# Sums of exponentials in free PSUM columns, pre-scaled keys, and a new order list, in an attention kernel with two feed-forward layers

## Chip, cores and metric

One core of one Trainium2 chip. The metric is the device time of one execution in microseconds; the median of the runs counts.

## What is computed

Attention over 2 batches of 8 heads, 768 positions of width 64, then two feed-forward layers on the 1536 rows of 512 that come out of it. Each query sees the keys less than 16 positions away, and besides them 24 summaries, one for each block of 32 keys (maximum of the keys, mean of the values):

```python
scale = 1.0 / np.sqrt(D)
k_sum = k.reshape(B, H, nb, block, D).max(axis=3)
v_sum = v.reshape(B, H, nb, block, D).mean(axis=3)
scores_l = scale * np.matmul(q, k.transpose(0, 1, 3, 2))
scores_s = scale * np.einsum('bhsd,bhnd->bhsn', q, k_sum) + np.log(block)
scores_all = np.concatenate([np.where(mask_l, scores_l, -1e9), scores_s], axis=-1)
a = np.exp(scores_all - np.max(scores_all, axis=-1, keepdims=True))
a = a / (np.sum(a, axis=-1, keepdims=True) + 1e-09)
x = np.matmul(a, np.concatenate([v, v_sum], axis=2))   # then heads side by side: 1536 x 512
h = x @ w_in;  x = (h * np.cos(h)) @ w_out              # first layer, 2048 wide
h = x @ w_in2; x = (h * np.clip(h + 3, 0, 6) / 6) @ w_out2
```

## The kernel before

The kernel is written as a graph of about 2,600 operations. `G.op` (L169) notes for each operation the engines that may do it, keys that it reads and writes, and a function that issues its instructions. `G.run` (L191) issues them in the order of `ORDER` (L39), a list written out in the file: `p118` puts operation 118 on TensorE's queue, `a` stands for ScalarE, `v` for VectorE, `g` for GpSimd, `s` for SP (which issues all DMAs). A `+2` puts two filler matmuls of zeros behind an operation (`fill`, L1028); `ws` and `we` load the tables for sine and exponential. Each engine works through its queue in order and waits there for what an instruction needs. The numbers are those of the graph, so a step that is added or removed renumbers what follows.

Attention runs in 12 units of 128 queries (`front`, L617, and `back`, L704). For a unit, with its 8 heads in two banks of PSUM (4 heads of 120 columns in each: 96 keys of the window, 24 summaries; 480 of a bank's 512 columns):

- masks (L633, an identity times the mask, on TensorE) or, from unit 7 on, a seed (a copy of the mask by ScalarE or VectorE, L443) fill the two banks; scores are added on top (L656; for units 0 to 3, called direct, straight from the keys, L658 and L660). Units 1 and 3 use banks a0 and a1, the others c0 and c1.
- largest (L684, VectorE): the maximum of each head; negative (L614 on VectorE, L612 on ScalarE): times minus the scale
- power (L693, ScalarE): eight exponentials of 120 columns, each with bias nmx and the scale, each followed by a reading of the accumulator into `sm`, which is the sum
- sum (L698), inverse (L700, both VectorE), scaled (L701, GpSimd or VectorE)
- flip (L723, transposes on TensorE), flipped (L443, a copy out of the bank), weighted (L739, times the values), x hi (L443) and x lo (L756): the result as two numbers of reduced precision
- units 0 and 1 take the first of these steps in two halves.

From unit 4 on the keys are not read from `ktile` but from `kcat`, into which window (L443) copies the keys of the unit's two windows and put k (L550) the summaries. The summaries of v are made by means (L579) and copied by put v (L443). Values of a window come by load window (L746).

The feed-forward layers take their weights as 64-bit floats; carry (L505, L507), rebias (L514), shift (L517), join (L519), hi (L443) and lo (L460) turn each slice of 512 KB into two 32-bit parts. A product is three matmuls (hi hi, hi lo, lo hi): first (L933) makes h, middle steps (L1009 to L1024) the gate, second (L1064) the second product. The first steps of the first layer run between the units of attention, 256 rows at a time; later steps take products in blocks (L881).

## Time and profile before

| | us |
|---|---|
| median of 3 runs | 569.22 (568.99 to 569.26) |
| the profiled execution, its own time | 570.81 |
| span of that execution, first to last instruction | 569.0 |
| TensorE busy in the span | 559.9 |
| VectorE / ScalarE / GpSimd busy | 460.6 / 341.4 / 231.3 |

Times of the trace are microseconds from the start of the span. PE is TensorE, PEld its weight loads, DVE is VectorE, ACT ScalarE, POOL GpSimd, SP SyncE. A busy TensorE is modelled from pipelined matmuls, so a matmul's row is longer than its share of the pipeline.

### The profile page before, as it was taken

The numbers are of one execution on the slowest core, as the hardware profiler recorded it, in microseconds if no ns is written. First come the engines' busy times: TensorE is split into PE (matmuls) and PEld (weight loads), VectorE is DVE, ScalarE is ACT, GpSimd is POOL, SyncE is SP. The second block draws the span as 40 slices with busy tenths as digits, with TensorE's granted clock in tenths as the row PEclk, the third lists the DMA queues.
The fourth block names the chain that finished last, engine by engine and source line by source line (L and its number), as shares of the span: only waits on it lengthen the run. The fifth ranks groups of instructions, "written<-read, shape, count | busy, mean of one in ns | idle before, by whom it ended". The sixth has DMA issues, their size and how long they took to land.

```text
span 569.0 us, 9914 instructions
## 1 busy us (share of the span) xinstructions
PE 559.9 (98%) x3736; PEld 477.4 (84%) x3736; DVE 460.6 (81%) x853; ACT 341.4 (60%) x730; POOL 231.3 (41%) x230
## 2 busy tenths in 40 slices
PE   9999999999999999999999999999999999999997
PEld 6688999888888888888888888888888889888885
DVE  5888897698999898978899998867778687766653
ACT  4989997757547786765668677655643443422130
POOL 4788756856524214435263453032132303132111
PEclk9999999999999999999999999999999999999999
DMA  8998525223012211233200222224203220200013
GB/s 299 285 259 279 161 67 177 76 74 101 11 39 74 75 38 38 75 116 105 75 2 0 75 74 75 75 74 149 74 7 130 87 74 2 75 1 1 29 46 149
DMA packets 17232, 51.49 MB, mean 90 GB/s; under 512 B 1952, under 2 KB 2464, under 8 KB 17184
## 3 DMA queue, kind: packets, MB, share of 16 engines
q1 hardware_dynamic: 17184, 50.86, 26.8%
q8 instruction: 29, 0.48, 0.3%
q14 instruction: 19, 0.16, 0.1%
HBM read 47.71 MB, written 3.15 MB: 89 GB/s over the span
## 4 chain that ended last, share of the span: by engine, by line
PE 92%; DMA 4%; DVE 2%; SPq 1%; issue 1%; ACT 0%; DVEq 0%; ACTq 0%
PE bank_a L1064 25%; PE bank_d L881 15%; PE bank_b L1064 11%; PE bank_c L1064 11%; PE bank_e L881 9%; PE bank_c L881 8%; PE bank_d L933 4%; PE bank_e L933 2%; DMA vcats<-in_vw_dram 2%; PE bank_c L933 1%; PE bank_b L739 1%; PE bank_b L723 1%; PE bank_c L656 1%; DMA raw<-in_w_in_dram 1%; DMA qt<-in_q_dram 1%
## 5 line engine op out<-in xcount | busy, mean ns | idle before, releaser
L514 ACT ACTIVATE cv_t<-raw 128x512 f32<-128x512 f32 x64 | 42.6, 674 | 21.2 <-POOL plo L460 7.6
L519 POOL TENSOR_TENSOR cv_y<-cv_t,cv_y 128x512 int32<-128x512 int32 x24 | 33.2, 1386 | 37.4 <-ACT cv_y L505 18.9
L443 ACT CAST ghi<-hs 128x512 fp32r<-128x512 f32 x44 | 27.2, 618 | 23.4 <-DVE hs L1020 12.8
L1024 POOL TENSOR_TENSOR glo<-ch_c,ghi 128x512 fp32r<-128x512 f32 x12 | 16.9, 1405 | 52.2 <-ACT ghi L443 43.9
L1024 DVE TENSOR_TENSOR glo<-hs,ghi 128x512 fp32r<-128x512 f32 x46 | 34.8, 758 | 3.4 <-ACT ghi L443 2.7
L505 ACT ACTIVATE cv_y<-raw 128x512 int32<-128x512 uint32 x47 | 31.0, 670 | 8.5 <-POOL plo L460 4.2
L517 DVE TENSOR_SCALAR cv_t<-cv_t 128x512 int32<-128x512 int32 x64 | 27.9, 440 | 4.1 <-ACT cv_t L514 3.8
L460 POOL TENSOR_TENSOR plo<-cv_y,phi 128x512 fp32r<-128x512 f32 (+1 forms) x15 | 17.2, 1150 | 32.2 <-ACT phi L443 32.1
L519 DVE CUSTOM_DVE_ANT_0 cv_y<-cv_t,cv_y 128x1024 uint16<-128x1024 uint16 x40 | 28.0, 706 | 1.2 <-ACT cv_y L505 1.1
L693 ACT ACTIVATE es<-bank_c,nmx 128x120 f32<-128x120 f32 x80 | 27.6, 370 | 1.9 <-DVE nmx L614 1.7
L881 PE MATMUL bank_d<-xlo,phi 128*128 128x256 f32 (+1 forms) x106 | 26.3, 329 | 0.0
L881 PE MATMUL bank_d<-xhi,plo 128*128 128x256 f32 (+1 forms) x106 | 26.2, 329 | 0.0
L881 PE MATMUL bank_d<-xhi,phi 128*128 128x256 f32 (+1 forms) x106 | 26.2, 328 | 0.0
L701 POOL TENSOR_TENSOR es<-es,rs 128x960 f32<-128x960 f32 (+1 forms) x14 | 21.9, 1565 | 9.1 <-DVE rs L700 8.5
L443 ACT CAST ghi<-ch_c 128x512 fp32r<-128x512 f32 x26 | 16.1, 618 | 12.9 <-DVE ch_c L1020 7.1
L897 DVE TENSOR_TENSOR ch_c<-bank_d,ch_c 128x256 f32<-128x256 f32 (+1 forms) x31 | 14.2, 462 | 10.4 <-PE bank_d L881 8.7
L1111 DVE SCALAR_TENSOR_TENSOR total<-bank_a,total 128x512 f32<-128x512 f32 x28 | 19.0, 686 | 3.3 <-PE bank_a L1064 3.3
L1024 POOL TENSOR_TENSOR glo<-hs,ghi 128x512 fp32r<-128x512 f32 x7 | 10.2, 1457 | 27.4 <-DVE ghi L443 12.4
L1064 PE MATMUL bank_a<-ghi,whi_out 128*128 128x512 f32 x60 | 21.3, 390 | 0.0
L1064 PE MATMUL bank_a<-ghi,wlo_out 128*128 128x512 f32 x60 | 21.3, 389 | 0.0
L1064 PE MATMUL bank_a<-glo,whi_out 128*128 128x512 f32 x60 | 21.2, 389 | 0.0
L881 PEld LDWEIGHTS bank_d<-xhi,phi 128*128 128x128 f32 x106 | 18.8, 189 | 2.8
(391 smaller groups left out, 1966.7 us busy)
## 6 DMA issues: line engine op xcount, KB each, us to landing
raw<-in_w_in_dram SPq DMA_DIRECT2D x32, 512.0 KB, 3.3
raw<-in_w_out_dram SPq DMA_DIRECT2D x32, 512.0 KB, 3.3
vcats<-in_vw_dram SPq DMA_DIRECT2D x12, 384.0 KB, 5.7
qt<-in_q_dram SPq DMA_DIRECT2D x12, 256.0 KB, 6.1
ktile<-in_kt_dram SPq DMA_DIRECT2D x7, 384.0 KB, 6.0
total<-in_vw_dram SPq DMA_DIRECT2D x8, 256.0 KB, 4.7
out_dram<-total SPq DMA_DIRECT2D x8, 256.0 KB, 2.1
vnat<-in_vw_dram SPq DMA_DIRECT2D x4, 256.0 KB, 5.5
```

Of the source, the lines that this page charges most:

```text
L443: nc.scalar.copy(o, i) if e == "ACT" else VEC[e].tensor_copy(o, i)
L505: nc.scalar.activation(y, low.bitcast(U32), AF.Copy, scale=2.0 ** -29)
L514: nc.scalar.activation(o, a, AF.Prelu, scale=2.0 ** -112, alpha=-2.0 ** 32)
L517: G.op("shift", {"DVE": dve(DM, 2)}, lambda e: nc.vector.tensor_scalar(t, t, 3, None, ALU.logical_shift_left), w=[tk], twice=True)
L519: G.op("join", {"POOL": pool(DM), "DVE": dve(DM)}, lambda e: VEC[e].tensor_tensor(y, t, y, ALU.add), r=[tk], w=[yk], twice=True)
L693: nc.scalar.activation(ef[:, j, hp], s4[j][:, hp, :], AF.Exp, bias=nmx[:, j, hp:hp + 1], scale=scale, accum_out=sm[:, j, hp:hp + 1])
L701: G.op("scaled", {"POOL": pool(2 * nz * KC, 1.25) - 0.07, "DVE": dve(2 * nz * KC)}, lambda e, ef=ef, rs=rs, nz=nz: VEC[e].tensor_tensor(ef ...
L881: nc.tensor.matmul(o, wt[i][:, A[a], kk * P:(kk + 1) * P], xt[:, kk, :], start=first and p + kk == 0, stop=p + kk == 3, skip_group_check=True)
L933: nc.tensor.matmul(h, w["in"][i][:, kk * P:(kk + 1) * P], x[blk][:, kk, c0:c1], start=p + kk == 0, stop=p == 2 and kk == NK - 1)
L1024: G.op("g lo", {"DVE": dve(N), "POOL": pool(N)}, lambda e: VEC[e].tensor_tensor(gbuf("lo", s)[:, 0:N], c(), gh().bitcast(F32), ALU.subtrac ...
L1064: nc.tensor.matmul(acc(s, i)[0], l, r, start=first, stop=end and p == 2 and (N == TOK or i % 2 == 1), skip_group_check=N < TOK)
L1111: G.op("sums", {"DVE": dve(TOK)}, lambda e: nc.vector.scalar_tensor_tensor(t(), a, 1.0 / 6.0 if m else 1.0, t(), ALU.mult, ALU.add), r=[ak ...
```

## The change

The scale of 1/8 moves. For units from 4 on the keys (window and put k), the seeds and the identity of the masks (`eighth`, `eighths`, two new tiles made by ScalarE) carry it; `largest` gives the negated maximum at once, `negative` is gone, and `power` uses scale 1. Units 0 to 3 keep their form. For all units `sm` is no longer a tile in SBUF: it is 8 columns of the second score bank, from column 480 + 8 x (unit modulo 2), so the accumulator's readings go to PSUM and `sum` reads them there. The keys of the graph for `sm` and for the bank stay separate. The graph has 2 operations more at the start and 8 fewer later, and `ORDER` is a new list. Its first lines, of 125 before and 124 after:

```diff
-    s6 p4 s5 s17 s7 g2 a3 a1 v11 s34 s9 p18+2 v10 s60 s8 v0 s283 p19 p35+3 v20 v12 a21 p36+1 s61 a22 v14 s290 v37 p66
-    s51 g119 v13 p26 a38 a39 p27+2 v23 v24 v284 s82 g25 v28 a285 p43 v29 p44 v286 s297 a30 v40 v287 p74 s62 p67+1 v45
-    g288 s64 p52 v31 a46 v75 g289 p53+1 s63 a47 v32 v41 s65 g33 a292 v54 p83 s99 g42 a299 p84 s78 v48 a55 v298 a56 v49
-    v300 p68 s95 g50 v85 p76 p69 p70+1 g101 v77 p71 s117 g15 p91 v86 g301 v72 a87 s311 p100 p102 g16 v57 v58 p79 v103
-    g59 a92 p93+2 v80 s113 a104 s138 a105 v94 g73 p109+2 v81 s136 g302 v110 p96 v293 v88 v303 s135 p111 a313 v89 p118
-    v312 a97 v314 p120 a112 v106 g315 v98 s137 a291 p114 v121 g90 s131 a316 p353 v142 a115 p365 p354 a122 s145 p366 p355
...
+    s8 p6+1 s7 s19 s10 s36 s11 s62 s9 g2 s277 v13 a4 a5 a3 s63 v12 a1 p20 s64 v0 p37 p21+2 s53 v22 s67 p38+1 v15 a23 a24
+    v39 p68+3 v16 v14 g103 a40 p28+1 a41 v25 v120 p29 v26 a278 p45 g27 v30 a279 p69 p46 v31 v42 s291 v280 a32 p70 v43
+    s84 v281 p76+2 s65 v47 g282 s66 a77 p54 s101 v44 a48 p55 s80 a49 g17 v283 g18 p93 v56 s118 a292 p85 s97 a293 p86 v33
+    v57 v34 s305 v294 a58 v35 p71 g295 v87 p72 p73 p78+3 v50 v88 v51 a296 g52 p102 a79 p104+5 v59 a89 g297 v74 v60 v105
+    p81 g61 p95+2 v94 a82 s114 v96 s284 g75 a106 p110+2 s137 v83 s136 v90 s138 p98 v91 v111 g92 p112 a99 s131 p119 v113
+    s135 a307 p347 s145 v100 p359 p348 p121 v306 v107 v308 v108 a285 g309 p115 v122 p360 a116 v310 p349 p361 v141 a286
...
```

Under the operations' names the queues are the same behind TensorE's 253rd, ScalarE's 321st, VectorE's 187th, GpSimd's 69th and SP's 51st operation of the new list. Ahead of that the places and, for some sixty operations, the engine differ. GpSimd has 12 operations fewer, ScalarE 6 more, VectorE as many as before. Where the steps below speak of one queue, these are its operations in their order, with the numbers of the old graph:

```text
SP before:    ... 61 load v, 290 weights, 51 load q, 82 load q, 297 weights, 62, 64, 63, 65 load v, 99 load q, 78, 95 load window,
              117 load q, 311 weights, 113 load window, 138, 136, 135, 137 load k, 131 load window, 145 load q, 304 weights, ...
SP after:     ... 61, 62 load v, 51 load q, 65 load v, 297 weights, 82 load q, 63, 64 load v, 99 load q, 78 load window, 117 load q,
              95 load window, 311 weights, 113 load window, 290 weights, 137, 136, 138 load k, 131 load window, 135 load k, ...
PE before:    ... 100 masks (unit 4), 102 scores, 79 weighted (unit 0), 93 flip+2, 109 flip+2, 96 weighted (unit 1), ...
PE after:     ... 76 flip+3, 100 masks (unit 4), 102 scores+5, 79 weighted (unit 0), 93 flip+2, 109 flip+2, 96 weighted (unit 1), ...
DVE before:   ... 85 largest, 77 flipped, 86 negative, 72 put v, 57 sum (unit 2), 58 inverse, 103 largest (unit 4), ...
DVE after:    ... 85 largest, 48 sum, 86 negative, 49 inverse, 57 sum (unit 2), 72 put v, 58 inverse, 103 largest (unit 4), ...
list after:   ... v57 behind p102;  v124 (sum, unit 5) between p146 and p148 (masks and scores, unit 6);
              v188 (sum, unit 8) behind a214 (seed, unit 9);  v238 (sum, unit 10) behind p252 (scores, unit 11) ...
```

The rest of the diff:

```diff
@@ -372,7 +371,7 @@
     qt = ring(kv, "qt", NQ, [P, HP, P])
     es = ring(kv, "es", NE, [P, 2, HP, KC])
     pts = ring(kv, "pts", 2, [KC, H, P])
-    small = {n: ring(kv, n, 2, [P, H]) for n in ("mx", "nmx", "sm", "sme", "rs")}
+    small = {n: ring(kv, n, 2, [P, H]) for n in ("mx", "nmx", "sme", "rs")}
 
 
     zero = const.tile([P, P], F32R, name="zero")
@@ -428,6 +427,10 @@
     both = [ident[:, c:c + QH].unsqueeze(1).to_broadcast([P, 2, QH]) for c in (0, QH)]
     G.op("identities", {"POOL": pool(P)}, lambda e: nc.gpsimd.tensor_tensor(
         twice.rearrange("p (a c) -> p a c", a=2), *both, ALU.add), w=["twice"], at=CONST, twice=True)
+    eighth = kv.tile([P, P], F32R, name="eighth")
+    eighths = kv.tile([P, P], F32R, name="eighths")
+    G.op("identity", {"ACT": act(P)}, lambda e: nc.scalar.mul(eighth, ident, scale), w=["eighth"], at=CONST)
+    G.op("identity", {"ACT": act(P)}, lambda e: nc.scalar.mul(eighths, twice.bitcast(F32), scale), r=["twice"], w=["eighths"], at=CONST)
     G.op("mask", {"ACT": act(3 * KC)}, lambda e: nc.scalar.copy(mask_hi, mask), w=["mask_hi"], at=CONST)
 
 
@@ -547,8 +550,8 @@
 
     def put_k(b, i):
         n = HP * 2 * NB
-        G.op("put k", {"DVE": dve(n, 2), "POOL": one(n)}, lambda e: VEC[e].tensor_copy(
-            kcat[i][:, :, :, WK:KC], ksum[b].unsqueeze(2).to_broadcast([P, HP, 2, NB])
+        G.op("put k", {"DVE": dve(n, 2), "POOL": one(n)}, lambda e: scaled_copy(
+            e, kcat[i][:, :, :, WK:KC], ksum[b].unsqueeze(2).to_broadcast([P, HP, 2, NB])
         ), r=[("ks", b, hp, c0) for hp, c0, _ in pieces(b)], w=[("kcs", i)], twice=True)
 
     def vstage(t):
@@ -612,6 +615,12 @@
             nc.scalar.activation(o, i, AF.Copy, scale=-scale)
         else:
             nc.vector.tensor_scalar(o, i, -scale, None, ALU.mult)
+
+    def scaled_copy(e, o, i):
+        if e == "ACT":
+            nc.scalar.activation(o, i, AF.Copy, scale=scale)
+        else:
+            VEC[e].tensor_scalar(o, i, scale, 1.0, ALU.mult, ALU.mult)
 
     def front(u):
         b, tb = divmod(u, TB)
@@ -627,22 +636,25 @@
             sp = [bank[n][:, 0:nz * KC] for n in spk]
             s4 = [x.rearrange("p (h c) -> p h c", h=nz) for x in sp]
 
-            def masks(e, sp=sp, nz=nz):
+            same = (twice if direct else eighths) if m == 1 else (ident_r if direct else eighth)
+
+            def masks(e, sp=sp, nz=nz, same=same):
                 for j in range(2):
                     js = slice(QH * j, QH * (j + 1)) if m == 1 else slice(0, P)
                     nc.tensor.matmul(
-                        sp[j], (twice if m == 1 else ident_r)[js], mask_hi[js, m, :].unsqueeze(1).to_broadcast(
+                        sp[j], same[js], mask_hi[js, m, :].unsqueeze(1).to_broadcast(
                             [js.stop - js.start, nz, KC]), start=True, stop=False)
 
             seeded = u >= SEEDED
             if seeded:
                 def seed(e, sp=sp, nz=nz):
                     for j in range(2):
-                        copy(e, sp[j].rearrange("p (h c) -> p h c", h=nz), mask_hi.bitcast(F32)[:, m, :].unsqueeze(1).to_broadcast([P, nz, KC]))
+                        scaled_copy(e, sp[j].rearrange("p (h c) -> p h c", h=nz), mask_hi.bitcast(F32)[:, m, :].unsqueeze(1).to_broadcast([P, nz, KC]))
 
                 G.op("seed", {"ACT": 2 * act(nz * KC), "DVE": 2 * dve(nz * KC)}, seed, r=["mask_hi"], w=spk)
             else:
-                G.op("masks", {"PE": 0.41 if m == 1 else 0.5}, masks, r=["mask_hi", "twice", "ident_r"], w=spk)
+                G.op("masks", {"PE": 0.41 if m == 1 else 0.5}, masks, r=["mask_hi", "twice", "ident_r"] if direct else [
+                    "mask_hi", "eighth", "eighths"], w=spk)
 
             def scores(e, s4=s4, z0=z0, z1=z1):
                 for part in range(2 if direct else 1):
@@ -668,33 +680,36 @@
                     ap=[list(ktile[0].ap[0]), [S, nz], [a[1] - a[0], 2], [1, WK]],
                 )
                 n = nz * 2 * WK
-                G.op("window", {"ACT": act(n), "DVE": 0.55, "POOL": one(n)}, lambda e, keys=keys: copy(
+                G.op("window", {"ACT": act(n), "DVE": 0.55, "POOL": one(n)}, lambda e, keys=keys: scaled_copy(
                     e, kc[:, :, :, 0:WK], keys), r=[x for hp in range(HP) for x in kkeys(hp)], w=[("kcw", k)], twice=True)
                 G.op("scores", {"PE": 0.98}, scores, r=[("qt", qi), ("kcs", k), ("kcw", k)], w=spk)
             ef = es[ei][:, :, z0:z1, :]
             gs = [g] if first else [0, 1]
-            mx, nmx, sm, sme, rs = (small[n][si].rearrange("p (j h) -> p j h", j=2)[:, :, z0:z1]
-                                    for n in ("mx", "nmx", "sm", "sme", "rs"))
+            mx, nmx, sme, rs = (small[n][si].rearrange("p (j h) -> p j h", j=2)[:, :, z0:z1]
+                                for n in ("mx", "nmx", "sme", "rs"))
+            c = HP * KC + H * si
+            sm = bank[spk[1]][:, c:c + H].rearrange("p (j h) -> p j h", j=2)[:, :, z0:z1]
 
             def key(n):
                 return [(n, si, x) for x in gs]
 
             def largest(e, mx=mx, s4=s4):
                 for j in range(2):
-                    nc.vector.tensor_reduce(mx[:, j], s4[j], AX.X, ALU.max)
-
-            G.op("largest", {"DVE": dve(2 * nz * KC) + 0.07}, largest, r=spk, w=key("max"))
-            G.op("negative", {"DVE": 0.1, "ACT": 0.2}, lambda e, nmx=nmx, mx=mx: negate(e, nmx, mx),
-                 r=key("max"), w=key("mx"), twice=True)
+                    nc.vector.tensor_reduce((mx if direct else nmx)[:, j], s4[j], AX.X, ALU.max, negate=not direct)
+
+            G.op("largest", {"DVE": dve(2 * nz * KC) + 0.07}, largest, r=spk, w=key("max" if direct else "mx"))
+            if direct:
+                G.op("negative", {"DVE": 0.1, "ACT": 0.2}, lambda e, nmx=nmx, mx=mx: negate(e, nmx, mx),
+                     r=key("max"), w=key("mx"), twice=True)
 
             def power(e, ef=ef, s4=s4, nmx=nmx, sm=sm, nz=nz):
                 for j in range(2):
                     for hp in range(nz):
-                        nc.scalar.activation(ef[:, j, hp], s4[j][:, hp, :], AF.Exp, bias=nmx[:, j, hp:hp + 1], scale=scale,
+                        nc.scalar.activation(ef[:, j, hp], s4[j][:, hp, :], AF.Exp, bias=nmx[:, j, hp:hp + 1], scale=scale if direct else 1.0,
                                              accum_out=sm[:, j, hp:hp + 1])
 
             ek = [("e", ei, x) for x in gs]
-            G.op("power", {"ACT": 2.75 * nz / HP}, power, r=key("mx") + spk, w=ek + key("sm"), table="exp")
+            G.op("power", {"ACT": 2.47 * nz / HP}, power, r=key("mx") + spk, w=ek + key("sm"), table="exp")
             G.op("sum", {"DVE": 0.13}, lambda e, sme=sme, sm=sm: nc.vector.tensor_scalar(sme, sm, 1.0e-9, None, ALU.add),
                  r=key("sm"), w=key("sme"), twice=True)
             G.op("inverse", {"DVE": 0.17}, lambda e, rs=rs, sme=sme: nc.vector.reciprocal(rs, sme), r=key("sme"), w=key("rs"))
```

## Rows read from the trace of the kernel before

**Rows 1.** Busy time, share of the span and instructions of each engine (page)

```profile
PE 559.9 (98%) x3736; PEld 477.4 (84%) x3736; DVE 460.6 (81%) x853; ACT 341.4 (60%) x730; POOL 231.3 (41%) x230
```

**Rows 2.** Table by stretches: length, busy us per engine (instructions), clock, DMA share, GB/s

```profile
core 0: us, PE busy (x) PEld busy (x) DVE busy (x) ACT busy (x) POOL busy (x), PEclk, DMA share, GB/s
...
20.00:30.00 10.00, 9.26 (x173) 6.90 (x169) 9.17 (x23) 9.13 (x46) 6.45 (x9) 1.00 0.91 265
30.00:40.00 10.00, 8.85 (x154) 7.98 (x143) 8.61 (x17) 8.55 (x29) 9.85 (x9) 1.00 0.90 248
...
60.00:70.00 10.00, 10.00 (x151) 9.24 (x151) 8.59 (x21) 9.21 (x34) 7.49 (x8) 1.00 0.38 126
...
160.00:300.00 140.00, 140.00 (x696) 118.97 (x695) 122.91 (x211) 93.08 (x160) 54.09 (x43) 1.00 0.19 65
```

**Rows 3.** TensorE's waits: who waited for whom, us in total, times, longest

```profile
PE bank_b L739 <- DMA vcats<-in_vw_dram: 1.1, 1, 1.1
...
PE bank_c L656 <- DMA qt<-in_q_dram: 0.8, 1, 0.8
PE bank_b L723 <- issue: 0.6, 1, 0.6
```

**Rows 4.** Groups by line and shape, 0 to 160 us: the filler matmuls

```profile
L1034 PE MATMUL bank_d<-zero 128*128 128x512 f32 x15 | 5.8, 448 | 0.0
```

**Rows 5.** The same view, ScalarE, VectorE and GpSimd: busy us, mean ns of one

```profile
L519 POOL TENSOR_TENSOR cv_y<-cv_t,cv_y 128x512 int32<-128x512 int32 x13 | 17.4, 1340 | 9.9 <-DVE cv_t L517 3.4 <-ACT cv_y L505 2.6 <-DVE sme L698 2.4
L693 ACT ACTIVATION_READ_ACCUMULATOR es<-bank_c,nmx 128x1 f32 x80 | 17.2, 216 | 0.0
...
L443 POOL COPY kcat<-ktile 128x768 f32<-128x768 f32 x8 | 6.6, 828 | 4.8 <-DMA ktile<-in_kt_dram 4.2 <-PE bank_c L656 0.5
...
L693 ACT ACTIVATION_READ_ACCUMULATOR es<-bank_a,nmx 128x1 f32 x16 | 3.4, 211 | 0.0
...
L443 ACT COPY bank_c<-mask_hi 128x480 f32<-128x480 f32 x6 | 3.2, 593 | 0.0
L443 ACT CAST ghi<-ch_c 128x512 fp32r<-128x512 f32 x5 | 3.1, 621 | 3.1 <-DVE ch_c L1015 2.4 <-PE bank_a L1064 0.7
...
L614 DVE TENSOR_SCALAR nmx<-mx 128x8 f32<-128x8 f32 x6 | 1.8, 298 | 0.1
...
L443 ACT CAST ghe<-ch_e 128x256 fp32r<-128x256 f32 x2 | 0.8, 404 | 0.0
```

**Rows 6.** ScalarE in order of time: start us, us, instruction

```profile
4.74 0.28 ACT L426 CAST ident_r<-ident 128x128 fp32r<-128x128 f32 x1
...
21.02 0.24 ACT L693 ACTIVATION_READ_ACCUMULATOR es<-bank_c,nmx 128x1 f32 x1
...
25.93 0.19 ACT L693 ACTIVATION_READ_ACCUMULATOR es<-bank_c,nmx 128x1 f32 x1
26.02 0.35 ACT L693 ACTIVATE es<-bank_c,nmx 128x120 f32<-128x120 f32 x1
```

**Rows 7.** VectorE in order of time

```profile
21.33 1.73 DVE L443 COPY vcats<-bank_e 24x256 f32<-24x256 f32 x4 [0.16 <-PE bank_e L579]
23.09 0.17 DVE L698 TENSOR_SCALAR sme<-sm 128x8 f32<-128x8 f32 x1
...
38.64 0.69 DVE L443 CAST xhi<-bank_b 128x512 fp32r<-128x512 f32 x1 [1.10 <-PE bank_b L739]
```

**Rows 8.** TensorE in order of time

```profile
22.55 0.48 PE L633 MATMUL bank_c<-mask_hi,twice 64*128 64x480 f32 x2
22.96 1.05 PE L656 MATMUL bank_c<-kcat,qt 64*64 64x120 f32 x32
23.94 1.15 PE L739 MATMUL bank_e<-pts,vcats 120*64 120x64 f32 x32
...
37.45 1.15 PE L739 MATMUL bank_b<-pts,vcats 120*64 120x64 f32 x32 [1.15 <-DMA vcats<-in_vw_dram]
```

**Rows 9.** The chain that ended last, in order of time: start us, us, what

```profile
28.36 8.95 DMA vcats<-in_vw_dram
...
76.90 0.96 PE bank_d L933 x8
```

More of the change, by code (lines that the diff above doesn't have):

```diff
@@ new lines @@
+    p1033 v972 p1036 v980 p1038 a973 p1035 a991 v974 p1037 v992 a998 p1046 a981 v1021 p1045 a993 v982 p1047 g994 a983
+    v1000 p1002 v1049 p1048 v1050 g984 a1003 a1025 v1051 p1004 a995 v1052 p1061 g1026 a1039 v1005 p1097 a1053 v1008
+    v1040 p1095 v1054 p1006 a1041 v996 p1098 v1007 a1060 v1023 p1096 a1055 v1022 v1042 p1105 a1029 p1009 v1024 v1062
+    p1063 v1056 a1031 v1030 p1064 a1043 v1010 a1057 p1066 g1044 a1111 p1106 a1027 v1067 p1107 a1080 v1032 p1109 a1099
+    v1058 p1108 a1075 v1070 p1110 v1112 p1068 v1100 a1113 p1071 v1069 v1081 p1118 a1123 v1114 p1120 a1101 v1028 p1117
@@ new lines @@
+    v1124 a1065 p1119 v1102 p1121 a1125 p1122 a1079 p1129 v1126 a1103 p1143 s1180 v1076 a1127 v1104 g1128 v1072 p1132
+    v1133 a1137 p1145 v1136 a1144 a1074 v1138 a1115 p1130 s1161 v1146 a1139 p1131 g1116 v1134 p1147 v1135 v1082 p1150
+    v1140 v1077 a1141 p1148 v1085 g1083 v1151 v1142 p1160 g1084 a1149 v1154 p1158 a1089 a1087 p1157 a1187 g1088 p1152
+    a1091 v1188 p1155 g1086 v1153 a1189 a1168 p1159 v1156 a1093 p1175 v1092 p1174 v1190 p1176 a1182 v1169 p1177 a1206
+    p1179 v1183 a1170 p1194 v1094 p1178 a1191 v1171 p1196 a1163 p1193 v1207 a1227 p1195 v1192 a1172 p1197 v1228 a1208
@@ new lines @@
+    p1212 p1198 v1209 p1247 v1216 a1210 p1245 v1173 a1181 p1215 v1164 a1229 s1220 v1211 p1213 a1246 g1230 v1219 p1233
+    v1217 p1214 g1090 p1236 v1218 a1231 p1240 a1162 v1184 p1235 v1232 s1199 a1222 g1165 v1244 p1234 a1185 v1248 p1238
+    g1186 a1166 p1239 v1242 p1237 v1243 g1167 p1252 a1201 p1250 v1223 a1221 v1253 a1200 p1249 v1241 s1264 a1251 v1202
+    p1295 s1259 v1256 v1224 p1294 v1203 p1254 a1225 a1204 p1257 g1226 p1298 v1258 v1255 p1299 v1302 a1281 p1293 v1205
+    a1287 p1296 v1282 a1266 v1288 p1297 a1283 v1267 p1305 a1289 v1301 g1284 v1303 p1307 v1290 a1306 a1285 a1261 p1300
```

226 lines of the change are left out of this document (105 added, 121 removed).

## The prediction

> **What bounds the kernel now.** I read four views, in this order. The busy times of the page put TensorE at 98% of the span and no other engine above 81% [rows 1]. The table by stretches says where the missing 2% lies: from 60 us on TensorE is busy 10.00 of 10 us and 140.00 of 140, while it loses 0.7 and 1.2 us in the two tens from 20 to 40 us [rows 2]. So the dense part runs at the pace of its matmuls, and the end moves by what TensorE loses, or stops losing, in the first 60 us or so. Its waits there are 1.1 us for a DMA into vcats, 0.8 for one into qt and 0.6 without a releaser [rows 3]. To these come 15 filler matmuls (5.8 us) that keep it running while attention is not ready [rows 4].
>
> Who paces that part? In the ten microseconds from 20 on VectorE is busy 9.17 and ScalarE 9.13, and the DMA engines 0.91 of the time [rows 2]: three resources near their limits. The page's average of 60% for ScalarE hides that.
>
> **What the change can reach.** I set the two order lists side by side, engine by engine, under the operations' names. All queues are the same from TensorE's 254th operation on; the part that differs is attention with the first feed-forward steps beside it. The TensorE work in it is the same set of operations apart from the fillers. So: new time = old time + change of TensorE's lost time in that part. The best that can happen is that 1.1 + 0.8 + 0.6 us of waits and some filler time go.
>
> **The change part by part** (units are blocks of 128 queries, 0 to 11).
>
> 1. *Negation, units 4 to 11.* Eight instructions go, three of them on ScalarE and five on VectorE (298 ns mean) [rows 5]. They stand between a unit's maximum and its exponentials, so each chain shortens by 0.2 to 0.3 us. Only units 4 to 6 fall where TensorE still waits, and what it waits for there is a DMA: value 0 (bounds -0.6, two chains, to 0).
>
> 2. *Sums into PSUM.* 96 readings of the accumulator, 211 to 216 ns each, get another destination [rows 5]. Does PSUM shorten one? The nearest rows: ScalarE writes 480 columns to PSUM in 593 ns and 512 to SBUF in 621; 256 to SBUF take 404, which is 0.85 ns a column, so 32 columns fewer give 594 [rows 5]. By these rows the destination costs and saves nothing: value 0. At most the reading's own slot could go, from its start at 25.93 to the next exponential's at 26.02 [rows 6]: 8 x 0.09 = 0.7 us per unit. The Trainium skill, "ScalarE: Activation LUTs", section "Step-by-step: what each stage is for", calls PSUM the lower-latency port of this engine. By it up to 0.7 us of unit 2's exponentials would go, and 0.7 of the sum below; the copies above don't bear it out.
>
> 3. *Scale on the key copies.* On GpSimd the window copy of 768 columns takes 828 ns; the new form multiplies. Bounds: 0.83 us (as a copy) to 768/512 x 1.34 = 2.0 us (as the join, which has two tensor operands) [rows 5]. Nearest is the copy, with one tensor operand. Unit 4's copy now heads GpSimd's queue, long before its use, so 1.2 us more is hidden; the later ones too, since 12 operations left that queue. Value 0; without the cover +1.2.
>
> 4. *Two more identities on ScalarE* stand around the mask and ahead of the plain identity, 2 x 0.28 us by the identity's row [rows 6]: unit 0's first scores start up to 0.5 us later. In exchange a carry leaves VectorE, where it stood ahead of a maximum of unit 0 and waited for its weights. Together 0.
>
> 5. *New queues.* On SP one 512 KB weight load moves from place 11 to 24, and the q, v and window loads behind it come earlier; the q of unit 7 now stands ahead of six v loads, where five preceded it. On TensorE 22 fillers stand before unit 1's weighted sum instead of 15: 7 x 0.39 = 2.7 us if nothing is awaited there [rows 4]. Five of them stand between unit 4's scores and unit 0's weighted sum, where TensorE must wait anyway (step 6): value 0.
>
> 6. *The added wait.* The sums lie in bank c1 (or a1), which the next unit's masks and scores write. In the new list unit 2's sum stands behind unit 4's scores. If a bank is given to one engine at a time, VectorE's sum of unit 2 waits for those scores; behind it in VectorE's queue stands put v, and unit 0's weighted sum waits for put v. Working: unit 2's last reading ends at 21.26, as before [rows 6]; masks 0.41 (22.55 to 22.96) and scores 0.98 (to 23.94) [rows 8] bring about 22.9 with gaps; sum 0.17 and put v 1.73 [rows 7] give 24.9 in place of 23.94: +1.0 us. Without the wait put v ends at 21.4 + 0.17 + 1.73 = 23.3, and fillers run up to 23.9: 0. No row of before has this wait: its sums are in SBUF. I take it, since the sums are read out of a bank that changes hands between engines for every unit. The Trainium skill, "PSUM — Partial Sum Buffer", section "PSUM bank collisions raise a hardware error", says that two engines at one bank and quadrant at once raise an error whatever the columns; by it the wait must be there. No row here shows it.
>
> 7. *The delay carried on.* Unit 0's weighted sum lets SP's next window load go; behind that stand four pieces of k and the window of unit 3, asked for at 28.36 and landed 8.95 us later, at 37.31 [rows 9]. TensorE starts unit 3's weighted sum at 37.45 [rows 8]. Now 512 KB of weights stand there in place of one 384 KB piece of k: 128 KB at 248 GB/s [rows 2] are 0.5 us. So it starts at 37.45 + 1.0 + 0.5 = 39.0. By then TensorE has done four more steps of the first layer (8 matmuls, 0.96 us [rows 9]) and lacks one pair of masks (0.41): +1.55 - 0.55 = +1.0.
>
> 8. *A second bank wait.* Unit 5's sum stands between unit 6's masks and scores, and on VectorE behind an x hi (0.69 us) that begins when unit 3's weighted sum ends [rows 7]. TensorE does the masks meanwhile and then waits: 0.04 + 0.69 + 0.17 - 0.41 = 0.5 us. Bounds 0 (no bank wait) to 0.5; value +0.5. Flips of unit 4 are queued behind it.
>
> 9. *Gain.* The 0.84 us wait for q goes with its earlier load: -0.84 [rows 3].
>
> Sum: 1.0 + 0.5 - 0.84 = +0.66 us. The profiled execution took 570.81 us for a span of 569.0, so 1.8 lie around it and stay: 571.5. On the median of 569.22 the same step gives 569.9.
>
> **The rivals.** *A, faster:* no wait on the bank, and the reading's slot shrinks by its whole bound for one unit. Steps 6 and 8 are 0, step 7 is 0.5 - 0.55, step 9 stays and step 2 gives -0.7: -1.6, so 567.6. For it: the order list was made from keys that hold sums and bank apart. Against: readers and writers share a bank, and the copies to PSUM are no shorter. *B, slower:* the bank waits also break the full busy time after 60 us. There VectorE is at 8.59 and ScalarE at 9.21 of ten [rows 2]. Unit 8's sum now stands behind ScalarE's seed of bank c1 (2 x 593 ns) and unit 10's behind unit 11's scores (0.98); each holds VectorE about 1 us, with flipped copies behind it that the in-order TensorE awaits. It decides where VectorE's slack of 0.14 us a microsecond is used up: +2.0 on top of 0.66, so 571.9. *C:* the parts cancel, and the new list only fills what it frees: 569.2.
>
> **How the numbers follow.** Forecast 0.42 (569.9; own range 569.0 to 570.9), A 0.21, B 0.29, C 0.08. About 0.2% (1.1 us) is what can be told from no change. Faster: 0.16 from A and 0.01 from the forecast, 0.17. Slower: 0.27 from B and 0.10 from the forecast, 0.37. The rest, 0.46, is the same. The range reaches to A and B: 567.6 to 571.9.
>
> **What the profile after would show.** Right: accumulator rows of L693 of unchanged length (step 2); VectorE's sum of unit 2 starting only when unit 4's scores end, and unit 0's weighted sum near 25; unit 3's near 39 behind a DMA; no wait for qt. Wrong: unit 0's weighted sum at 24 or earlier (A); accumulator rows much shorter (step 2); GpSimd's window rows near 2 us (step 3); TensorE waits between 60 and 95 us (B).

## The result, and the profile after

The changed kernel takes 578.53 us (median of 6 runs, 578.07 to 580.88) against 569.52 us for the kernel before in the same set (6 runs, 568.99 to 572.62): a ratio of 1.015, with an interval of 1.0127 to 1.0173. It is 9 us slower; the forecast was 569.9 us, with a range that ended at 571.9. The profiled execution took 578.08 us for a span of 576.3, so again 1.8 us lie around the span, and all of the change lies in it.

The busy times and the chain that ended last, from the page of after:

```profile
PE 564.4 (98%) x3743; PEld 479.4 (83%) x3743; DVE 461.2 (80%) x854; ACT 348.9 (61%) x735; POOL 224.6 (39%) x218
...
PE 84%; ACT 10%; DVE 4%; issue 1%; POOL 1%; DVEq 0%; POOLq 0%; ACTq 0%
```

The shares hardly moved [rows 1]; in us TensorE is busy 4.5 longer and ScalarE 7.5. The chain did move: ScalarE holds 10% of it now. Where, the table by stretches says (us busy per engine, clock, DMA share, GB/s); first after, then before for the last four tens:

```profile
40.00:50.00 10.00, 9.41 (x142) 8.22 (x140) 9.23 (x20) 9.41 (x21) 7.79 (x8) 1.00 0.49 154
50.00:60.00 10.00, 9.21 (x158) 8.41 (x157) 8.63 (x21) 9.65 (x30) 5.66 (x6) 1.00 0.96 324
60.00:70.00 10.00, 9.45 (x124) 8.67 (x122) 7.23 (x15) 9.62 (x32) 8.97 (x11) 1.00 0.47 153
70.00:80.00 10.00, 8.55 (x137) 7.56 (x137) 8.36 (x20) 9.28 (x28) 6.18 (x7) 1.00 0.43 146
80.00:90.00 10.00, 9.68 (x149) 8.88 (x146) 9.34 (x19) 9.72 (x31) 7.41 (x6) 1.00 0.30 97
90.00:100.00 10.00, 9.44 (x101) 8.98 (x100) 7.00 (x17) 9.68 (x27) 6.53 (x9) 1.00 0.29 91
100.00:110.00 10.00, 10.00 (x83) 8.72 (x82) 5.97 (x8) 5.71 (x10) 6.03 (x6) 1.00 0.42 139
```

```profile
70.00:80.00 10.00, 10.00 (x133) 9.64 (x131) 9.26 (x22) 9.96 (x36) 6.69 (x8) 1.00 0.41 128
80.00:90.00 10.00, 10.00 (x153) 9.44 (x152) 9.13 (x21) 9.16 (x29) 5.26 (x5) 1.00 0.40 127
90.00:100.00 10.00, 10.00 (x92) 9.10 (x91) 6.82 (x14) 5.92 (x11) 6.47 (x7) 1.00 0.37 127
```

Read the first and the fourth busy column. Before, TensorE is full from 60 us on and ScalarE is done with attention soon after 90 (5.92). After, TensorE loses 0.55, 1.45, 0.32 and 0.56 us in the four tens from 60 to 100, and ScalarE is at 9.3 to 9.7 of ten right up to 100. The clock is 1.00 in all of them. Of the 7.3 us that the span grew by, 2.8 are idle time of TensorE and 4.5 are in its modelled busy time; 1.7 of these are fillers (step 5 below), and the rest was not traced further. TensorE's waits (who waited for whom, us in total, times, longest, 0 to 110 us of after):

```profile
PE bank_b L754 <- ACT pts L446: 1.4, 2, 0.8
PE bank_b L738 <- ACT pts L446: 1.1, 2, 0.6
...
PE bank_e L754 <- DVE vcats L446: 0.8, 1, 0.8
PE bank_c L668 <- ACT bank_c L621: 0.5, 2, 0.3
...
PE bank_c L668 <- DVE sme L713: 0.3, 1, 0.3
```

The waits for DMAs into qt and vcats [rows 3] are gone; of the rows shown, three of five wait for ScalarE, the two largest among them. What ScalarE does longer is in its order of time (start us, us). First after, from the exponentials of one late unit:

```profile
58.14 0.34 ACT L708 ACTIVATE es<-bank_c,nmx 128x120 f32<-128x120 f32 x1
58.38 0.16 ACT L708 ACTIVATION_READ_ACCUMULATOR es<-bank_c,nmx 128x1 f32 x1
58.58 0.36 ACT L708 ACTIVATE es<-bank_c,nmx 128x120 f32<-128x120 f32 x1
58.84 0.16 ACT L708 ACTIVATION_READ_ACCUMULATOR es<-bank_c,nmx 128x1 f32 x1
59.03 0.36 ACT L708 ACTIVATE es<-bank_c,nmx 128x120 f32<-128x120 f32 x1
...
92.98 0.16 ACT L708 ACTIVATION_READ_ACCUMULATOR es<-bank_c,nmx 128x1 f32 x1
```

and the last reading of before:

```profile
85.62 0.24 ACT L693 ACTIVATION_READ_ACCUMULATOR es<-bank_c,nmx 128x1 f32 x1
```

The reading of the accumulator is shorter, 0.16 us where it was 0.19 to 0.24 [rows 6]. But look at the starts. Before, the next exponential starts at 26.02, 0.10 us ahead of the end of the reading that began at 25.93 and takes 0.19 [rows 6]; the two overlap. After, it starts at 58.58, 0.03 to 0.04 us behind the end of the reading. Start to start, the exponentials of a unit are 0.336 us apart before and 0.455 after (the median within each unit; 0.454 to 0.457 over the units). A unit of eight takes 2.85 us before and 3.61 after, a half unit of four 1.48 and 1.79. Over the kernel the exponentials hold ScalarE 4 x 0.31 + 10 x 0.76 = 8.8 us longer, and its last one ends at 93.15 in place of 85.86, 7.3 us later, which is just what the span of the two profiled executions grew by (the medians are 9.0 apart; the profiled execution of before, 570.81, was one of its longer ones). In the profiles of all the runs below, too, the span ends 482.3 to 483.8 us after the last exponential, so the end moves with the end of attention.

### The profile page after: what moved, and what is told of

Its sections match the earlier page's. It is cut to its first block, busy times and chain, and to the rows that moved or that the text cites. A ratio compares the mean times of both kernels' runs of the same rounds, so it can differ in the third digit from the quotient of the medians.

```text
span 576.3 us, 9921 instructions
## 1 busy us (share of the span) xinstructions
PE 564.4 (98%) x3743; PEld 479.4 (83%) x3743; DVE 461.2 (80%) x854; ACT 348.9 (61%) x735; POOL 224.6 (39%) x218
## 4 chain that ended last, share of the span: by engine, by line
PE 84%; ACT 10%; DVE 4%; issue 1%; POOL 1%; DVEq 0%; POOLq 0%; ACTq 0%
PE bank_a L1079 21%; PE bank_d L896 15%; PE bank_b L1079 10%; PE bank_c L1079 10%; PE bank_e L896 9%; PE bank_c L896 8%; ACT es L708 5%; PE bank_d L948 3%; PE bank_e L948 1%; PE bank_c L948 1%; ACT L1165 1%; DVE total L1126 1%; ACT ch_e L1028 1%; PE bank_b L738 1%; PE bank_c L668 1%
## 5 line engine op out<-in xcount | busy, mean ns | idle before, releaser
L522 POOL TENSOR_TENSOR cv_y<-cv_t,cv_y 128x512 int32<-128x512 int32 x26 | 36.1, 1392 | 42.5 <-ACT cv_y L508 18.9
L508 ACT ACTIVATE cv_y<-raw 128x512 int32<-128x512 uint32 x51 | 33.7, 669 | 8.6 <-POOL plo L463 4.2
L1039 POOL TENSOR_TENSOR glo<-ch_c,ghi 128x512 fp32r<-128x512 f32 x11 | 15.6, 1415 | 50.4 <-ACT ghi L446 42.1
L463 POOL TENSOR_TENSOR plo<-cv_y,phi 128x512 fp32r<-128x512 f32 (+1 forms) x16 | 19.3, 1205 | 36.1 <-ACT phi L446 35.6
L708 ACT ACTIVATE es<-bank_c,nmx 128x120 f32<-128x120 f32 x80 | 28.9, 361 | 2.8 <-DVE nmx L698 0.5
L522 DVE CUSTOM_DVE_ANT_0 cv_y<-cv_t,cv_y 128x1024 uint16<-128x1024 uint16 x38 | 26.4, 702 | 1.2 <-ACT cv_y L508 1.1
L716 POOL TENSOR_TENSOR es<-es,rs 128x960 f32<-128x960 f32 (+1 forms) x12 | 19.9, 1658 | 11.6 <-DVE rs L715 11.6
L463 POOL TENSOR_TENSOR wlo_out<-cv_y,whi_out 128x512 fp32r<-128x512 f32 x12 | 15.8, 1317 | 14.2 <-ACT whi_out L446 11.4
```

Of the source, the lines that this page charges most:

```text
L463: G.op("lo", {"POOL": pool(n), "DVE": dve(n)}, lambda e: VEC[e].tensor_tensor(lo(), x, hi().bitcast(F32), ALU.subtract), r=[*r, hk[0]], w= ...
L508: nc.scalar.activation(y, low.bitcast(U32), AF.Copy, scale=2.0 ** -29)
L522: G.op("join", {"POOL": pool(DM), "DVE": dve(DM)}, lambda e: VEC[e].tensor_tensor(y, t, y, ALU.add), r=[tk], w=[yk], twice=True)
L708: nc.scalar.activation(ef[:, j, hp], s4[j][:, hp, :], AF.Exp, bias=nmx[:, j, hp:hp + 1], scale=scale if direct else 1.0, accum_out=sm[:, j ...
L1039: G.op("g lo", {"DVE": dve(N), "POOL": pool(N)}, lambda e: VEC[e].tensor_tensor(gbuf("lo", s)[:, 0:N], c(), gh().bitcast(F32), ALU.subtrac ...
```

## The experiments

I began with two theories from the profile after. Theory 1: VectorE's waits for the bank ahead of its sums (rival B's mechanism) make the loss. Theory 2: the new list makes it, which hands ScalarE more work. Ratios are to runs of the kernel before in the same set, with 95% intervals. Besides the ratio the text gives, where they bear on it, the spacing of the exponentials (start to start within a unit, from ScalarE's rows) and the end of the last exponential's reading.

### The sums back in SBUF, in the new list

```diff
...
-            mx, nmx, sme, rs = (small[n][si].rearrange("p (j h) -> p j h", j=2)[:, :, z0:z1]
-                                for n in ("mx", "nmx", "sme", "rs"))
-            c = HP * KC + H * si
-            sm = bank[spk[1]][:, c:c + H].rearrange("p (j h) -> p j h", j=2)[:, :, z0:z1]
+            mx, nmx, sm, sme, rs = (small[n][si].rearrange("p (j h) -> p j h", j=2)[:, :, z0:z1]
+                                    for n in ("mx", "nmx", "sm", "sme", "rs"))
```

> The changed kernel with its new order list, but the sums of the exponentials in an SBUF tile again. Theory 1 (bank waits): VectorE's sums stand in the list behind the next scores of their bank, and the 9.1 us that VectorE idles before its sums in the first 110 us are the loss; then this runs in 569 to 571 us, with VectorE idle under 2 us before the sums, although ScalarE's 96 readings are back near 216 ns. Theory 2 (the list): the new list gave ScalarE 4.6 us more work in the first 100 us (82.8 to 87.4 us busy) and ScalarE sets the end of attention; then this stays at 577 to 581 us, the upper end since the readings take longer again.

Measured: 571.33 us, ratio 1.0009 (0.9990 to 1.0028). Spacing 0.336 us, last end 87.00. The place of the sums is the whole loss; the new list, the scale and the negated maxima together cost nothing that can be told from before. Theory 2 falls as it was put. VectorE's idle time before its sums fell to 1.8 us, as theory 1 had it, but the run takes away two things at once: the wait of VectorE for the bank, and the wider spacing on ScalarE.

### The whole change in the old list

```diff
 ORDER = """
-    (the changed kernel's list)
+    (the list of before, the eight negations left out, the two identities behind the plain one)
```

> All code of the change (sums in PSUM, scale on the keys, negated maxima) in the order of the kernel before (the eight negations left out, the two new identities behind the plain one). Theory 1 (bank waits): in this order too 10 of the 14 sums stand behind the next masks, seed or scores of their bank, so VectorE waits before its sums, 5 us or more, and the time is 572 to 578 us. Theory 2 (the list): the old list was right and the shorter readings are a gain: 566 to 570 us.

Measured: 574.04 us, ratio 1.0052 (1.0034 to 1.0071). Spacing 0.455 us, last end 89.84. The sums in PSUM make the old list slower too, so the change as written can't be saved by its order alone; but the old list loses about a third of what the new one does (0.52% against 1.50%; against the same list with the sums in SBUF, below for the old one, half: 0.73% against 1.41%).

### The old list with the sums in SBUF

The edits of the two kernels above together: what is left of the change is the scale on the keys and the negated maxima.

> The order of the kernel before, sums in SBUF, only the scale on the keys and the negated maxima kept. Theory 1 and theory 2 both: 568 to 570 us, no difference from the kernel before. A third theory (the new instructions themselves are dearer: the GpSimd copies that multiply, the two identities) gives 572 us or more. The readings show whether their length hangs on the destination: 216 ns if so, 165 if it hangs on the scale of 1.

Measured: 570.01 us, ratio 0.9979 (0.9954 to 1.0003). Spacing 0.336 us, the readings in the c banks back at 218 ns, last end 84.75. The new instructions are not dearer (theory 3 of the text above falls), and the shorter reading came with the sums in PSUM, not with the scale. What makes it shorter the runs below take apart.

### Each sum ahead of the next scores of its bank

In the list ten of the fourteen sums move; unit 2's is `v59`, unit 4's masks and scores are `p102` and `p104`:

```diff
-    a296 g52 p102 a79 p104+5 v59 a89
+    a296 g52 v59 p102 a79 p104+5 a89
```

> The changed kernel and its new list, but each sum that stood behind the next masks, seed or scores of its bank is moved directly ahead of them, so that VectorE's sum waits for the exponentials alone. Theory 1 (bank waits): VectorE's idle time before the sums falls from 9.1 to under 4 us and the time to 567 to 571 us. Theory 2 (the list): 576 to 579 us.

Measured: 577.62 us, ratio 1.0116 (1.0092 to 1.0141). Spacing 0.455 us, last end 93.09. The sum's row in the groups of VectorE (busy us, mean ns | idle before it, and what ended it), first of the changed kernel, then of this one:

```profile
L713 DVE TENSOR_SCALAR sme<-bank_c 128x8 f32<-128x8 f32 x9 | 1.5, 164 | 9.1 <-PE bank_c L668 4.3 <-ACT es L708 2.9 <-ACT bank_c L621 1.9
```

```profile
L720 DVE TENSOR_SCALAR sme<-bank_c 128x8 f32<-128x8 f32 x9 | 1.5, 165 | 7.0 <-ACT es L715 7.0
```

No sum of these waits for TensorE's scores or for a seed any more, and nothing is won that can be told (1.0116 and 1.015, the intervals overlap): VectorE stands idle 7.0 us for the exponentials instead. The next user of the bank was only the last of several things that these sums wait for, and behind it stood ScalarE, which sets the end of attention as late as before (93.09). Theory 1 is in doubt, so I formed another.

**Theory 4, own waits.** The instruction lists of the two programs, as built from the two kernels, show a wait that no view of the trace names, since ScalarE waits for itself (the four exponentials of one unit that read the pair's second bank; first after, then before):

```
L708 ACTIVATE es_132,bank_c_97<-bank_c_97,nmx_137 128x120 [waits Activation_49] x4
L693 ACTIVATE es_132,sm_139<-bank_c_97,nmx_137 128x120 [waits PE_49]
L693 ACTIVATE es_132,sm_139<-bank_c_97,nmx_137 128x120 x3
```

All four wait for ScalarE's own semaphore in the changed kernel, and in the kernel before only the first waits, for TensorE. Over the kernel 85 of the 96 exponentials wait for the instruction just ahead of them; in the new list with the sums in SBUF 3 do. The program orders all that touches one PSUM bank by the bank, not by the columns: with the sum written into that bank, each exponential has to wait until the one ahead of it has put its sum there. Against it stood theory 5: writing a sum to PSUM takes ScalarE longer by itself.

### The own wait alone, with the sums in SBUF

```diff
+                last = None
                 for j in range(2):
                     for hp in range(nz):
-                        nc.scalar.activation(ef[:, j, hp], ..., accum_out=sm[:, j, hp:hp + 1])
+                        made = nc.scalar.activation(ef[:, j, hp], ..., accum_out=sm[:, j, hp:hp + 1])
+                        if last is not None:
+                            G.behind(made, last)
+                        last = made
```

> The new list with the sums in SBUF (571.3 us in the first set, the exponentials of a unit 0.336 us apart), and one thing added: each exponential of a unit waits for the end of the one ahead of it, as it does in the changed kernel, where each sum is written into the bank that the next one touches. Theory 4 (own waits): ScalarE's wait for its own last sum is what spaces the exponentials 0.455 us in the changed kernel, 2.85 to 3.61 us a unit, 4 x 0.31 + 10 x 0.76 = 8.8 us over all, and this is the loss; then they are 0.44 us apart or more here too, and the time is 576 to 580 us. Theory 5 (the destination): writing a sum to PSUM takes ScalarE longer by itself; then the spacing stays near 0.336 and the time near 571 us.

Measured: 579.53 us, ratio 1.0176 (1.0143 to 1.0210). Last end 94.41. ScalarE in order of time:

```profile
58.84 0.34 ACT L707 ACTIVATE es<-bank_c,nmx 128x120 f32<-128x120 f32 x1
59.09 0.19 ACT L707 ACTIVATION_READ_ACCUMULATOR es<-bank_c,nmx 128x1 f32 x1
59.31 0.36 ACT L707 ACTIVATE es<-bank_c,nmx 128x120 f32<-128x120 f32 x1
```

The next exponential starts at 59.31, 0.03 us behind the end of the reading at 59.28, as in the changed kernel, though nothing of the sums is in PSUM. Start to start it is 0.484 us. The wait alone brings the whole loss. The spacing is even 0.029 us wider than in the changed kernel, since a reading into SBUF takes 0.19 us where one into PSUM takes 0.16; that this makes the kernel slower than the changed one is not shown (the intervals overlap). Theory 4 stands.

### The sums in two banks, taken in turn

```diff
-            sm = bank[spk[1]][:, c:c + H].rearrange("p (j h) -> p j h", j=2)[:, :, z0:z1]
+            sm = [bank[n][:, c + z0:c + z1] for n in spk]
...
-                for j in range(2):
-                    for hp in range(nz):
+                for hp in range(nz):
+                    for j in range(2):
...
-                                             accum_out=sm[:, j, hp:hp + 1])
+                                             accum_out=sm[j][:, hp:hp + 1])
...
-            ... nc.vector.tensor_scalar(sme, sm, 1.0e-9, None, ALU.add)
+            ... [nc.vector.tensor_scalar(sme[:, j], sm[j], 1.0e-9, None, ALU.add) for j in range(2)]
```

> The changed kernel with its new list and its sums in PSUM, but the sums of the scores in the first bank of a pair lie in the first bank, those of the second in the second, and the exponentials take the banks in turn: a sum is then never in the bank that the next exponential reads or writes, and the wait is for the one before the last. VectorE adds two instructions in place of one per sum (14 x 0.15 us more). Theory 4 (own waits): spacing 0.28 to 0.34 us and 569 to 573 us. Theory 5 (the destination): spacing 0.455 us and 577 to 580 us. Theory 1 (VectorE's bank waits): whatever the spacing, 575 us or more, since these waits stay.

Measured: 572.15 us, ratio 1.0046 (1.0019 to 1.0072). Last end 86.35.

```profile
55.99 0.34 ACT L708 ACTIVATE es<-bank_c,nmx 128x120 f32<-128x120 f32 x1
56.23 0.16 ACT L708 ACTIVATION_READ_ACCUMULATOR es<-bank_c,nmx 128x1 f32 x1
56.28 0.36 ACT L708 ACTIVATE es<-bank_c,nmx 128x120 f32<-128x120 f32 x1
56.52 0.18 ACT L708 ACTIVATION_READ_ACCUMULATOR es<-bank_c,nmx 128x1 f32 x1
```

All sums are in PSUM, and the exponentials are 0.295 us apart: the reading and the next exponential overlap again, and the spacing is 0.041 us shorter than with sums in SBUF. Most exponentials wait for ScalarE here too (68 of 96), but for the one before the last, and that costs nothing that shows. Theory 5 falls, and theory 1, which had 575 us or more here, is out by 3 us. The four spacings make a table:

| | waits for the one ahead | does not |
|---|---|---|
| sums in SBUF | 0.484 | 0.336 |
| sums in PSUM | 0.455 | 0.295 |

PSUM saves 0.03 to 0.04 us an exponential; the wait costs 0.15 to 0.16. The two-bank kernel also takes the banks in turn, which the other three don't; turn-taking with sums in SBUF was not run.

### VectorE's bank wait alone

```diff
-            ... nc.vector.tensor_scalar(sme, sm, 1.0e-9, None, ALU.add)
+            ... nc.vector.scalar_tensor_tensor(sme, x, 0.0, sm, ALU.mult, ALU.add)
```

where `sm` is in SBUF and `x` are columns of the scores' bank that hold zeros (cleared once at the start).

> The new list with the sums in SBUF, and VectorE's sum also takes a column of the scores' bank (times 0), so that it waits for the bank as in the changed kernel while ScalarE is free of its own waits. Theory 1 (VectorE's bank waits): 574 to 578 us. Theory 4 (own waits of ScalarE): 570 to 573 us, as without the bank waits, with VectorE idle before the sums for a few us that cost nothing.

Measured: 572.22 us, ratio 1.0033 (1.0020 to 1.0047). Spacing 0.336 us, last end 87.32.

```profile
L713 DVE SCALAR_TENSOR_TENSOR sme<-bank_c,sm 128x8 f32<-128x8 f32 x9 | 1.4, 160 | 5.2 <-PE bank_c L670 3.4 <-ACT bank_c L623 1.2 <-ACT es L708 0.6
```

VectorE stands idle 5.2 us before these sums, nearly all of it for scores and seeds, and the time is 1.4 us (0.24%) above the same kernel without it (1.0009); the two intervals overlap. (The 5.2 us are less than the 9.1 of the changed kernel, where the exponentials themselves come later.) Theory 1 falls as the cause of the 9 us.

### Only the sums in PSUM, nothing else of the change

The kernel before and its list; the one edit is the first diff of this section, the other way round.

> The kernel before and its order list, with only the sums moved into PSUM; scale and negations as they were. Theory 4 (own waits): exponentials 0.455 us apart, ScalarE 8.8 us more in attention, of which the old list, where ScalarE had idle time (9.09, 9.21 and 9.16 of ten from 50, 60 and 80 us), hides a part: ratio to before 1.003 to 1.009, as with all of the change in the old list (1.0052). If the scale and the negations paid for some of it there, this is 1.009 or more.

Measured: 577.01 us, ratio 1.0120 (1.0097 to 1.0143). Spacing 0.455 us, last end 91.75. One part of the change, alone, costs 6.8 us in the old list. With the scale and the negated maxima beside it the old list loses less (1.0052), the second branch of what was expected: these two parts together are worth nothing that can be told with the sums in SBUF (0.9979, its interval takes in 1), and some 4 us with the sums in PSUM. Which of the two parts it is, and how these 4 us come about, was not traced further.

### The own wait for the later units alone

```diff
-                        if last is not None:
+                        if last is not None and u >= 6:
```

> The new list with the sums in SBUF and the added own wait of ScalarE, but only for the exponentials of units 6 to 11 (6 x 0.97 = 5.8 us of the 11.5 us that it adds over all units, which cost 1.0176 to before against 1.0009 without it). Theory 4 with ScalarE as the pace of late attention (9.3 to 9.9 of ten busy from 40 us on): nearly all of the 5.8 us shows, ratio 1.008 to 1.012. If instead the delay arises in the first units and is only carried on, this is 1.001 to 1.004.

Measured: 576.18 us, ratio 1.0126 (1.0088 to 1.0163). Last end 91.01. 5.8 us more on ScalarE from 45 us on move the end by (1.0126 - 1.0009) x 570 = 6.7 us (by the interval of this run 4.5 to 8.8): most or all of it shows. (In the profiled executions the last exponential ends 4.0 us later than without the wait, 91.01 and 87.00.) From 45 us to the end of attention ScalarE has little slack to hide it, and the delay is not one that is made in the first units and carried on.

### Two banks in turn, in the old list

The diff of the two banks above, with the old list.

> The whole change with the sums in the bank of their own scores and the banks in turn, in the order of the kernel before. In the new list this gave exponentials 0.295 us apart and 1.0046. Theory 4: the same spacing here (10 x 0.24 + 4 x 0.12 = 2.9 us less on ScalarE than with sums in SBUF), and as the old list stood 0.3% better than the new one with the sums in SBUF (0.9979 to 1.0009), a ratio of 0.997 to 1.002. If VectorE's bank waits decide here, 1.004 or more.

Measured: 569.16 us against 570.25 for before in this set, ratio 0.9986 (0.9973 to 0.9999). Spacing 0.295 us, last end 84.70. This form keeps all three parts of the change and undoes the harm: 9 us faster than the changed kernel by the ratios, and 0.1% ahead of the kernel before, which is less than can be told apart with confidence. TensorE is at 10.00 of ten in every ten microseconds from 50 to 100 us here, so the 2.9 us that ScalarE needs less (10 x 0.24 + 4 x 0.12) would have nothing left to shorten there.

### Two banks in turn, sums ahead of the next scores

> As the run before this one in the set, and each sum that stood behind the next masks, seed or scores of its bank is put directly ahead of them. If VectorE's bank waits still cost some tenths of a per cent with ScalarE's own waits gone, this is faster than with the sums where they stood: ratio 0.993 to 0.999. If they cost nothing, both are the same.

Old list: 574.13 us, ratio 1.0073 (1.0043 to 1.0103). I had expected a gain or nothing. The table by stretches of its profiled execution, from 10 to 40 us, TensorE's waits, and the first two of them in its order of time:

```profile
10.00:15.00 5.00, 3.83 (x71) 2.57 (x75) 4.64 (x15) 3.67 (x21) 1.37 (x3) 0.90 0.81 309
15.00:20.00 5.00, 5.00 (x79) 3.38 (x75) 1.69 (x7) 2.99 (x13) 3.76 (x4) 0.50 1.00 339
20.00:25.00 5.00, 4.33 (x95) 3.36 (x91) 2.08 (x7) 2.84 (x17) 2.30 (x4) 0.50 1.04 307
25.00:30.00 5.00, 4.20 (x52) 2.36 (x46) 3.26 (x8) 2.22 (x15) 1.38 (x2) 0.73 0.10 40
30.00:35.00 5.00, 4.34 (x69) 3.74 (x70) 2.23 (x7) 2.02 (x12) 3.43 (x3) 0.66 0.02 5
35.00:40.00 5.00, 4.90 (x82) 3.71 (x80) 4.86 (x14) 3.94 (x16) 0.66 (x1) 1.00 0.77 254
```

```profile
PE bank_c L651 <- DVE sme L720: 2.8, 3, 1.5
PE bank_a L651 <- DVE sme L720: 1.2, 2, 0.7
```

```profile
11.34 0.49 PE L651 MATMUL bank_c<-mask_hi,ident_r 128*128 128x240 f32 x2 [0.62 <-DVE sme L720]
...
13.74 0.47 PE L651 MATMUL bank_a<-mask_hi,twice 64*128 64x240 f32 x2 [0.56 <-DVE sme L720]
```

Now the masks wait for the sum: 4.0 us in five waits, up to 1.5 us, four of them in the first 31 us. Behind the first two (they end at 11.3 and 13.7 us) the granted clock, the third column from the end, goes from 1.00 to 0.50 (from 2.4 to 1.2 GHz) and is back for good only at 35 us; the same kernel with the sums where they stood has 1.00 throughout. This profile is of the slowest of the five executions. Their mean clocks and times are 1.000 at 572.74 and 573.05, 0.997 at 574.13, 0.991 at 576.49 and 0.985 at 579.70: without a fall of the clock the move costs some 3.7 us (572.9 against 569.16 with the sums where they stood), and where the clock falls up to 7 more.

> The new list, sums in the bank of their own scores with the banks in turn, and each sum directly ahead of the next masks, seed or scores of its bank. Against the same without that move (1.0046): if VectorE's bank waits are what keeps it above the kernel with the sums in SBUF (1.0009), 0.997 to 1.002; if the second VectorE instruction of each sum or the list is, 1.003 to 1.006.

New list: 571.62 us, ratio 1.0034 (1.0017 to 1.0051), last end 86.11; without the move it was 1.0046. The intervals overlap, so moving the sums decides nothing here either. Whether the new list stays above the same list with sums in SBUF (1.0009) is not clear of noise, and what would keep it 0.2 to 0.4% above stays open between the list, the second VectorE instruction and the bank waits.

## Why the prediction was wrong, step by step

**Step 2 failed: the sums into PSUM were costed at nothing.** I asked only whether the accumulator's reading would change its length, took the copies into PSUM and SBUF [rows 5] as the nearest rows, and left room for a gain of 0.7 us a unit and for no loss. Measured: the exponentials 0.455 us apart in place of 0.336, +0.76 us a unit, 8.8 us over the kernel. The copies were the wrong neighbours: none of them writes a bank that the next instruction on its engine reads. That what shares a bank waits, I had written down myself for VectorE and TensorE (step 6), and did not apply to ScalarE against itself. The rows that could have priced it stood in front of me: a reading begins at 25.93 and takes 0.19, and the next exponential begins at 26.02 [rows 6]. There are 82 such neighbours (7 in each of ten units, 3 in each of four half units). A wait would take the overlap of 0.10 us from each and leave the gap of 0.03 behind the reading, 10.7 us; a reading 0.03 us shorter brings that to 8.2, near the 8.8 measured. The sign that I had named for this step, much shorter readings, did come (165 ns where 216 stood [rows 5]), but beside a longer slot: I had taken the row for the cost.

The rule that I weighed there, that PSUM is the lower-latency port of ScalarE (the Trainium skill, "ScalarE: Activation LUTs", section "Step-by-step: what each stage is for"), agrees with the runs: 0.295 us in place of 0.336 in the two-bank run, which also takes the banks in turn, and 0.455 in place of 0.484 where each waits. By the first, 8 x 0.041 = 0.33 us a unit, about half of the bound of 0.7. It was the wait that turned the sign.

**And the second half of step 2's cost: there was no cover.** Even with +0.76 us a unit the end would not move if ScalarE had slack. The stretches give it 9.1 of ten in the twenties [rows 2], and the same table reads 9.96 and 9.16 for 70 to 90 us of before (shown above). I named ScalarE as near its limit ahead of the steps and then worked out slack for VectorE alone. With it fell the frame of the sum, that nothing is lost after 60 us: TensorE idles 2.9 us in the four tens from 60 to 100.

**Steps 6 and 7: the mechanism was right, the size was off, through step 2.** Unit 2's sum stands behind unit 4's scores, put v behind the sum, unit 0's weighted sum behind put v (VectorE, then TensorE, in order of time):

```profile
24.34 0.17 DVE L713 TENSOR_SCALAR sme<-bank_c 128x8 f32<-128x8 f32 x1 [2.71 <-PE bank_c L668]
24.54 1.73 DVE L446 COPY vcats<-bank_e 24x256 f32<-24x256 f32 x4
```

```profile
26.32 1.15 PE L754 MATMUL bank_e<-pts,vcats 120*64 120x64 f32 x32 [0.76 <-DVE vcats L446]
...
41.17 1.15 PE L754 MATMUL bank_b<-pts,vcats 120*64 120x64 f32 x32 [0.59 <-ACT pts L446]
```

In the program's list this sum waits for TensorE's semaphore, so the added wait of step 6 is there, put in by the program. The weighted sum starts at 26.32; forecast 24.9 (the step's own terms add to 24.8), before 23.94 [rows 8]. Unit 2's exponentials end at 22.68 in place of 21.27, and that 1.4 us is the rest. Unit 3's comes at 41.17, not 39.0, and it waits for ScalarE, not for a DMA: step 7's chain of loads was no longer the last to arrive. By the run with VectorE's bank wait alone, all bank waits of this kind are worth 1.4 us, not clear of noise; steps 6 and 8 had 1.5.

**Step 8** is there and small: TensorE waits 0.3 us for VectorE's sums, forecast 0.5. **Step 9** is right: no wait for qt is left. **Step 3** is right, and its near row was the good one: the window copy that multiplies takes 834 ns, 828 as a plain copy [rows 5]; the copies of the key maxima onto kcat went unpriced and take 560 ns in place of 345, four of them, hidden. **Step 4** is right, 0.30 us each, and unit 0's exponentials start at 8.85 in place of 8.65. Groups by line and shape of after:

```profile
L1049 PE MATMUL bank_d<-zero 128*128 128x512 f32 x22 | 7.5, 430 | 0.0
...
L623 POOL TENSOR_SCALAR kcat<-ktile 128x768 f32<-128x768 f32 x6 | 5.0, 834 | 8.5 <-DMA raw<-in_w_in_dram 4.8 <-PE bank_c L668 3.6
L623 POOL TENSOR_SCALAR kcat<-ksum 128x192 f32<-128x192 f32 x4 | 2.2, 560 | 0.3 <-DVE ksum L547 0.3
...
L432 ACT ACTIVATE eighth<-ident 128x128 fp32r<-128x128 f32 x1 | 0.3, 303 | 0.0
```

**Step 5**: the 22 fillers take 7.5 us where 15 took 5.8 [rows 4], 1.7 us more, beside TensorE's waits for attention. The new queues were costed at nothing, and with the sums in SBUF they are (1.0009). With the sums in PSUM they are not: the new list loses 1.015 where the old one loses 1.0052, perhaps because it gives ScalarE other work besides (9 carries in place of 5 up to 110 us) just where its exponentials grow; no run shows that reason. **Step 1**, the negations at 0, agrees with the sums in SBUF (0.9979 in the old list, with the scale); with the sums in PSUM the two parts together are worth some 4 us.

**Rival B** named the place (TensorE waits between 60 and 95 us) and the sign, with the wrong engine and 571.9 us where 578.5 was measured: VectorE's bank waits there could be taken away (sums ahead of the next scores) and the time stayed at 1.0116. **Rival A** needed no wait on the bank, and VectorE waits 9.1 us for banks and for what writes them; its other half, the shorter slot of the reading, is real, but only where ScalarE doesn't wait for itself.
